# An adaLN block with a long convolution and a spatial gating MLP on one core: where the operand sets of the spatial product are built, stored and loaded

## The chip, the cores and the metric

The kernel runs on one core of a Trainium2 chip. The metric is the device time of one execution in microseconds; lower is better. Engines are named as in the profile: PE is TensorE's matmuls and PEld its weight loads, DVE is VectorE, ACT is ScalarE, POOL is GpSimd, SP is SyncE. SP, ACT and POOL also issue DMAs, each in its own queue, in order.

## The reference, cut to what matters

```python
x = A_u                                             # [1, 2048, 576], f32
sa, ca, ga, sb, cb, gb = (silu(c) @ w_mod), six rows of 576
h = layernorm(x) * (1 + ca) + sa
x = x + ga * ssm_convolution(h)                     # 128 states a channel, by FFT in the reference
h = layernorm(x) * (1 + cb) + sb
z = gelu(h @ w_in)                                  # w_in 576 x 4608
z1, z2 = z[:, :2304], layernorm(z[:, 2304:])
g = w_sp @ z2 + b_sp[:, None]                       # w_sp 2048 x 2048, the spatial product
x = x + gb * ((z1 * g) @ w_out)                     # w_out 2304 x 576
```

The change lies in the second half, from the second layernorm on.

## The kernel before, in words

**Numbers.** Each f32 operand of the large matmuls is split into two fp16 parts, hi and lo, and three products of parts stand for one product. Large products are made by a Strassen-like scheme with seven products of half-sized blocks in place of eight. It needs seven combined operands on either side, sums and differences of four quarter blocks, each as hi and lo.

**First stage (`phase_a`).** All 2048 rows, in 16 tiles b of 128, go through the second layernorm, are transposed on TensorE (`turn`), and multiplied with the z2 half of w_in (`z2_mm`, five column parts h). ScalarE applies the gelu (`z2_gelu`), statistics follow, the normalised z2 is stored to `z2_d` in HBM. The transposed tile lies in PSUM (`pt`, two banks, one buffer). `turn_hi` (ACT) and `turn_lo` (DVE) make its fp16 parts. For b of 4 and more `turn_lo` also copies all of it in f32 with ScalarE to `nf` (a single buffer, shown as `wf` in the profile) and stores that with three POOL DMAs to `nm_d` and `nr_d`, for the later blocks. In this stage every instruction keeps its written order on its engine (`self.nc = self.tied`).

**Second stage (`phase_b`).** Four blocks q of 512 output rows each. A block has nine units f of 256 columns of z. A unit makes z1 (`z1_unit` in block 0, `z1_pair` in blocks 1 to 3) and then the spatial product (`g_unit`, `g_products`) over four operand sets n = 4f to 4f+3 of z2, each multiplied with two of the eight tiles of w_sp of the block. A set has 14 fp16 tiles, 896 KB, in a ring of three buffers (`zset`). It takes 42 matmuls: for each of two w_sp tiles seven products of three parts, one part on each of lines L1586, L1587 and L1588. After the nine units DVE scales and adds the bias (`gt`), multiplies with z1, and `out_block` multiplies with w_out (L1638 to L1641).

**Operand sets.** `set_unit` either builds a set from z2 (`z2_build`: a load of 512 KB from `z2_d` on SP into `raw`, three sums on DVE, then hi on ACT, L1136, and lo on DVE, L1137, twice each) or loads it ready from `set_d` with a POOL DMA (L1563). `kept_in(n)` is 1 for every third set and 0 else. A set with 0 is built in block 0, stored to `set_d` by an ACT DMA (L1580) and loaded in blocks 1 to 3. A set with 1 is built in block 0 and again in block 1, stored in block 1, and loaded in blocks 2 and 3. `ready(q, n + 2)` asks for a set when set n starts.

**w_in's combined operands.** Blocks 1 to 3 need the z1 half of w_in as seven combined operands for each f (`wc`, `wcr`, one buffer each). `w_load(f)` reads w_in on SP into two `raw` buffers; `w_build(f)` makes them (eight sums and three lo parts on DVE, three hi parts on ACT) and stores them with two POOL DMAs (L1523, L1524) to `wc_d` and `wr_d`. In block 1 `w_build(f + 1)` follows `z1_pair(1, f)`; blocks 2 and 3 load them (`w_parts`). `w_load(0)` stands at the end of unit 7 of block 0, `w_build(0)` and `w_load(1)` in its unit 8, after `n_build` (which makes the combined operands of the transposed rows) and ahead of `g_unit(0, 8)`.

**w_sp of the next block.** `wsp_read` loads eight tiles of 512 KB on SP into `raw` (four buffers, shared by z2, w_in, w_sp, w_out, the transposed rows and x), `wsp_build` combines them, between the last unit and `out_block`.

**Order.** The kernel's framework schedules instructions on each engine itself, except where the helper `Mixed` or `tied` keeps the written order: SP always, DVE and ACT in unit 8 of blocks 0 to 2 and from the fourth `wsp_build` on. Lines of such instructions show as L133. POOL is never tied in this stage.

Of the kernel before, what the change touches and what calls it, by code (L numbers as in the profile page):

```python
# [800 lines left out]
class Mlp:  # L801
# [409 lines left out]
        A.activation(nt[:, 8], pm[:, 1, :128], AF.Copy)  # L1211

    def turn_lo(self, b):
        V, pm, nt = self.nc.vector, self.tps.pop(b), self.nts[b]
        V.tensor_tensor(nt[:, 4:8], pm[:, 0].rearrange("p (k c) -> p k c", k=4), nt[:, 0:4], op=ALU.subtract)
        V.tensor_tensor(nt[64:, 8], pm[64:, 1, :128], nt[64:, 8], op=ALU.subtract)
        if b < 4:
            self.nc.gpsimd.dma_start(self.n2_d[:, b], nt)
            return
        q, t, c = b // 4 - 1, b % 4 // 2, slice(128 * (b % 2), 128 * (b % 2) + 128)  # L1220
        nf = self.nf
        self.nc.scalar.activation(nf, pm.rearrange("p k n -> p (k n)")[:, :640], AF.Copy)
        self.nc.gpsimd.dma_start(self.nm_d[q, t, :, :, c], nf[:, :512].rearrange("p (k c) -> p k c", k=4))
        for h in range(2):
            self.nc.gpsimd.dma_start(self.nr_d[q, :, 2 * t + h, c], nf[32 * h:32 * h + 32, 512:])
# [39 lines left out]
    def phase_a(self):  # L1265
# [21 lines left out]
        def do(b, k):  # L1287
            for fn, a in sides[b][k]:
                fn(*a)
# [65 lines left out]
        for b in range(1, 16):  # L1355
            do(b, LD)
            self.z2_mm(b, 0)
            do(b, A0)
            self.z2_gelu(b, 0)
            self.z2_stats(b - 1, 5)  # L1360
            if b in (1, 2):
                do(b, PE)
                self.z2_mm(b, 1)
                self.turn(b + 1)
                self.z2_gelu(b, 1)
                self.turn_hi(b + 1)
                self.turn_lo(b + 1)
            self.roots(b - 1, b + 2 if b + 2 < 16 else None)
            if b % 2:
                self.z2_diff(b - 1)  # L1370
            self.z2_norm(b - 1)
            if b + 2 < 16:
                self.ln2_rows(b + 2)
            if b + 4 < 16:
                self.x1_load(b + 4)
            if b > 2:
                if b > 3:
                    do(b, PE)
                self.z2_mm(b, 1)
                if b + 1 < 16:  # L1380
                    self.turn(b + 1)
                self.z2_gelu(b, 1)
            self.z2_store(b - 1)
            do(b, V0)
            self.z2_stats(b, 0, 1)
            if 3 < b + 1 < 16:
                self.turn_hi(b + 1)
                self.turn_lo(b + 1)
            self.z2_mm(b, 2)
            if b == 3:  # L1390
                do(b, PE)
            self.z2_gelu(b, 2)
            do(b, A1)
            self.z2_mm(b, 3)
            self.z2_stats(b, 2, 3)
            self.z2_gelu(b, 3)
            if b + 3 < 16:
                self.ln2_stats(b + 3)
            do(b, V1)
            self.z2_stats(b, 4)  # L1400
            self.z2_mm(b, 4)
            self.z2_gelu(b, 4)
# [154 lines left out]

    def set_unit(self, n, q):

        if q <= self.kept_in(n):  # L1560
            return self.z2_build(n)
        o = self.bp.tile([128, 7, 2, 256], F16, name="zset", bufs=3)
        self.nc.gpsimd.dma_start(o, self.set_d[n // 4, n % 4])  # L1563
        return o

    def kept_in(self, n):
        return 1 if n % 3 == 2 else 0

    def g_products(self, q, f):

        T = self.nc.tensor
        p6, p32, p17, p54 = pg = [self.bank().rearrange("p (k n) -> p k n", k=2) for _ in range(4)]

        todo = [(5, 4, p6, 0), (6, 1, p32, 0), (3, 2, p32, 1), (1, 0, p17, 0), (0, 5, p17, 1), (4, 3, p54, 0), (2, 6, p54, 1)]
        for i in range(8):
            if i % 2 == 0:
                n = 4 * f + i // 2
                z = self.zset.pop((q, n))
                if q == self.kept_in(n):
                    self.nc.scalar.dma_start(self.set_d[f, i // 2], z)  # L1580
                self.ahead(q, n)
            w = self.wsp[q, i]
            c = slice(128 * (i % 2), 128 * (i % 2) + 128)
            for a, b, bank, half in todo:
                pm = bank[:, half]
                T.matmul(pm, z[:, a, 0, c], w[:, b, 0], start=i + half == 0, stop=False, skip_group_check=True)  # L1586
                T.matmul(pm, z[:, a, 0, c], w[:, b, 1], start=False, stop=False, skip_group_check=True)  # L1587
                T.matmul(pm, z[:, a, 1, c], w[:, b, 0], start=False, stop=i == 7, skip_group_check=True)  # L1588
        return pg
# [94 lines left out]
    def phase_b(self):  # L1684
# [2 lines left out]
        self.pb = self.pool(self.ctx, "pb", 8, space=PSUM)  # L1687
        self.bank = lambda: self.pb.tile([128, 512], F32, name="ps")
        self.zset = {}
        made = [n for n in range(36)], [n for n in range(36) if self.kept_in(n)], [], []  # L1690
        loaded = [0] * 4
        AHEAD = 3

        def more(q, n):

            while loaded[q] < min(n, len(made[q])):
                self.z2_load(made[q][loaded[q]])
                loaded[q] += 1

        def ready(q, n):  # L1700
            if n < 36:
                if n in made[q]:
                    more(q, made[q].index(n) + (AHEAD if q == 0 else 1))
                self.zset[q, n] = self.set_unit(n, q)

        blocks = [0] * 4
# [31 lines left out]
        bp.tile([128, 7, 2, 256], F16, name="zset", bufs=3)  # L1738
        bp.tile([128, D], F32, name="gbs")
        bp.tile([128, 288], F32, name="ot", bufs=2)  # L1740
        more(0, AHEAD)
        self.wsp_read(self.raw(("b", 7)), 0, 7)
        ready(0, 0)
        for i in range(2, 6):
# [4 lines left out]
        for q in range(4):  # L1749
            done = 0  # L1750

            def z1(n):
                nonlocal done
                while done < min(n, 18):
                    self.z1_unit(q, order[done])
                    done += 1

            for f in range(9):
                if f == 8 and q < 3:
                    self.scales_sp(q + 1, self.bank())  # L1760
                    self.scales_gate(q + 1)
                if q == 0:
                    if f == 5:
                        self.scales_in(self.bank())
                    z1(units(q, f))
                else:
                    self.z1_pair(q, f)
                    if q == 1 and f < 8:
                        self.w_build(f + 1)
                        if f < 7:  # L1770
                            self.w_load(f + 2)
                    elif q > 1 and f < 8:
                        self.w_parts(f + 1)
                if f == 8 and q < 3:
                    if q == 0:
                        self.cfp.close()
                        self.parts_open()
                    self.nc, plain = Mixed(self.tc, self.tied, self.tied), self.nc
                    self.n_build()
                    if q == 0:  # L1780
                        self.w_build(0)
                        self.w_load(1)
                    else:
                        self.w_parts(0)
                    self.nc = plain
                self.g_unit(q, f)
                if q == 0:
                    if f == 5:
                        for i in (6, 7):
                            self.wsp_load(1, i, None)  # L1790
                            self.norm_sp(1, i)
                elif q < 3 and f < 6:
                    for i in ((0, 1), (2, 3), (4,), (5,), (6,), (7,))[f]:
                        self.wsp_load(q + 1, i, None)
                        self.norm_sp(q + 1, i)
                if f == 6 and q < 3:
                    self.sums_sp(q + 1)
                if f == 6:
                    self.load_gate(q)
                if q == 0 and f == 3:  # L1800
                    self.sums_in()
                if f == 7 and q < 3:
                    self.n_load(q + 1)
                    if q == 0:
                        self.w_load(0)
            self.scale_gate(q)
            if q < 3:
                for i in range(8):
                    if i == 3:
                        self.nc, plain = Mixed(self.tc, self.tied, self.tied), self.nc  # L1810
                    self.wsp_build(q + 1, i)
                    block(q + 1, i + 5)
                self.nc = plain
                self.bias_load(q + 1)
                ready(q + 1, 0)
                ready(q + 1, 1)
            self.out_block(q)
# [85 lines left out]
```

## Time and profile before

| | us |
|---|---|
| median of 3 runs | 1806.05 |
| lowest and highest | 1804.48, 1806.15 |
| profiled execution | 1803.76 |
| its span | 1801.9 |

| engine | busy in the span |
|---|---|
| PE | 1690.0 us, 94% |
| PEld | 1255.6 us, 70% |
| DVE | 1253.0 us, 70% |
| ACT | 848.0 us, 47% |
| POOL | 246.8 us, 14% |

Within the span, the first stage of the MLP ends near 690 us. The spatial products of the four blocks start at 694.76, 971.74, 1270.22 and 1536.76 us. An x and a number behind a busy time is the count of instructions. "Idle before" is how long an engine stood still just ahead of an instruction, and the arrow names what ended that. The granted clock is TensorE's, 1.00 being full speed.

### The profile page before, as it was taken

Reading aid. Unit: us, or ns where it says so; the run is one execution under the profiler, and the core shown is the slowest. Engines: PE = TensorE matmul, PEld = TensorE weight load, DVE = VectorE, ACT = ScalarE, POOL = GpSimd, SP = SyncE. Lnnn points to the kernel's source line nnn. Section 1 sums busy time; section 2 is a strip of 40 time slices with the busy share of each in tenths; the row PEclk is TensorE's granted clock in tenths of the full one; section 3 lists DMA queues with packets and bytes.
Section 4 is the critical chain, followed back from the end, with each engine's and each line's share of the span. In section 5 each row is a group of like instructions: output and inputs, shape, how many; then the busy total and the mean of one; then the engine's idle time right before and its main releaser. Section 6 shows DMA issues by size and latency. Waiting matters only on the chain. (4 is left out here: it accounts for less than half of the span.)

```text
span 1801.9 us, 35541 instructions
## 1 busy us (share of the span) xinstructions
PE 1690.0 (94%) x14771; PEld 1255.6 (70%) x14771; DVE 1253.0 (70%) x2365; ACT 848.0 (47%) x1084; POOL 246.8 (14%) x392
## 2 busy tenths in 40 slices
PE   5687999997999999999989889899999999999999
PEld 1344555564545547777767778787888887888887
DVE  6997999866888888996976658687344467344432
ACT  4778999944577675554532434343122133111110
POOL 2221222332133220000000001000000000000000
PEclk9898999997999999999999999999999999999999
DMA  8457455799598788876545567673666682555620
GB/s 274 141 201 250 133 140 167 196 252 284 177 301 272 243 238 270 296 278 225 191 168 202 211 261 255 253 269 122 214 227 225 216 285 76 181 210 195 234 91 27
DMA packets 148368, 380.67 MB, mean 211 GB/s; under 512 B 24160, under 2 KB 61984, under 8 KB 146672
## 3 DMA queue, kind: packets, MB, share of 16 engines
q1 hardware_dynamic: 103104, 176.49, 31.4%
q0 software_dynamic: 35616, 163.76, 26.9%
q10 hardware_dynamic: 9488, 38.16, 5.2%
q8 instruction: 116, 1.90, 0.4%
q14 instruction: 44, 0.36, 0.1%
HBM read 266.05 MB, written 102.86 MB: 205 GB/s over the span
## 5 line engine op out<-in xcount | busy, mean ns | idle before, releaser
L1586 PE MATMUL ps<-wsp,zset 128*128 128x256 f16 x2016 | 553.5, 275 | 22.4 <-ACT zset L1136 13.9
L1588 PE MATMUL ps<-wsp,zset 128*128 128x256 f16 x2016 | 552.1, 274 | 3.2 <-DVE zset L1137 3.2
L1587 PE MATMUL ps<-wsp,zset 128*128 128x256 f16 x2016 | 553.1, 274 | 0.0
L1586 PEld LDWEIGHTS <-zset 128*128 128x128 f16 x2016 | 198.7, 99 | 50.4 <-ACT zset L1136 16.2
L133 PE MATMUL pz<-wz,nt 128*128 128x512 f16 (+1 forms) x1120 | 224.0, 360 | 2.3 <-ACT nt L133 1.9
L1588 PEld LDWEIGHTS <-zset 128*128 128x128 f16 x2016 | 198.4, 98 | 29.2 <-DVE zset L1137 5.1
L1587 PEld LDWEIGHTS <-zset 128*128 128x128 f16 x2016 | 198.7, 99 | 25.0
L1601 DVE SCALAR_TENSOR_TENSOR gt<-ps,sc,bsp 128x512 f32<-128x512 f32 x33 | 24.8, 750 | 251.9 <-PE ps L1588 251.9
L133 PEld LDWEIGHTS <-nt 128*128 128x128 f16 x1120 | 109.6, 99 | 108.4 <-ACT nt L133 3.5
L1563 POOL DMA_DIRECT2D zset<-set_d x96 | 50.8, 529 | 835.3 <-PE ps L1588 580.3
L1638 PE MATMUL ps<-wout,z 128*128 128x288 f16 x448 | 125.4, 289 | 6.7 <-DVE gt L133 4.7
L1640 PE MATMUL ps<-wout,z 128*128 128x288 f16 x448 | 128.3, 289 | 1.4 <-DVE gt L133 1.4
L1641 PE MATMUL ps<-wout,z 128*128 128x288 f16 x448 | 128.3, 289 | 0.0
L1550 ACT ACTIVATE z<-ps 128x512 f32<-128x512 f32 x21 | 12.5, 597 | 229.6 <-PE ps L1543 229.6
L1601 DVE SCALAR_TENSOR_TENSOR gt<-ps,sc,gt 128x512 f32<-128x512 f32 (+1 forms) x165 | 112.0, 696 | 5.2 <-DVE gt L1601 0.5
L1540 PE MATMUL ps<-nq,wc 128*128 128x256 f16 x378 | 103.1, 273 | 0.0
L1542 PE MATMUL ps<-nq,wc 128*128 128x256 f16 x378 | 103.1, 273 | 0.0
L1541 PE MATMUL ps<-nq,wc 128*128 128x256 f16 x378 | 102.9, 272 | 0.0
L1136 ACT ACTIVATE zset<-raw 128x1024 f16<-128x1024 f32 x48 | 50.3, 1050 | 98.1 <-DMA raw<-z_d 33.7
L1137 DVE TENSOR_TENSOR zset<-raw,zset 128x1024 f16<-128x1024 f32 x48 | 58.7, 1223 | 29.5 <-ACT zset L1136 29.5
L133 DVE BATCH_NORM_STATS2 bsz<-z 128x6 f32<-128x384 f32 x96 | 48.5, 547 | 17.3 <-ACT z L133 17.3
L1640 PEld LDWEIGHTS <-z 128*128 128x128 f16 x448 | 44.2, 99 | 18.0 <-DVE gt L133 6.6
(410 smaller groups left out, 3374.6 us busy)
## 6 DMA issues: line engine op xcount, KB each, us to landing
zset<-set_d POOLq DMA_DIRECT2D x96, 896.0 KB, 4.9
set_d<-zset ACTq DMA_DIRECT2D x36, 896.0 KB, 6.2
raw<-z_d SPq DMA_DIRECT2D x48, 512.0 KB, 5.0
raw<-in_w_spT SPq DMA_DIRECT2D x43, 512.0 KB, 5.8
z_d<-z POOLq DMA_DIRECT2D x32, 576.0 KB, 7.8
wc<-wc_d SPq DMA_DIRECT2D x18, 896.0 KB, 4.8
u_d<-st1o POOLq DMA_DIRECT2D x16, 576.0 KB, 4.8
u<-u_d SPq DMA_DIRECT2D x36, 256.0 KB, 4.8
```

Source lines behind the costliest of these rows:

```text
L133: return self.tc.keep_in_program_order(f(*a, **k))
L1137: nc.vector.tensor_tensor(o[:, k, 1], t, o[:, k, 0], op=ALU.subtract)
L1540: T.matmul(pm, w[0], n[0], start=c + half == 0, stop=False, skip_group_check=True)
L1541: T.matmul(pm, w[0], n[1], start=False, stop=False, skip_group_check=True)
L1542: T.matmul(pm, w[1], n[0], start=False, stop=False, skip_group_check=True)
L1586: T.matmul(pm, z[:, a, 0, c], w[:, b, 0], start=i + half == 0, stop=False, skip_group_check=True)
L1587: T.matmul(pm, z[:, a, 0, c], w[:, b, 1], start=False, stop=False, skip_group_check=True)
L1588: T.matmul(pm, z[:, a, 1, c], w[:, b, 0], start=False, stop=i == 7, skip_group_check=True)
L1601: V.scalar_tensor_tensor(dst, pm, inv, to, op0=ALU.mult, op1=ALU.add)
L1638: T.matmul(pl, p[:, 1, ts], w[:, 0, hs], start=st, stop=sp)
L1640: T.matmul(pa, p[:, 0, ts], w[:, 0, hs], start=st, stop=False)
L1641: T.matmul(pa, p[:, 0, ts], w[:, 1, hs], start=False, stop=sp)
```

## The change

`set_unit` builds sets in block 0 only, all 36 are stored there by ACT DMAs, and blocks 1 to 3 load all of theirs with POOL DMAs; `kept_in` goes. `w_load(0)`, `w_build(0)` and `w_load(1)` move from units 7 and 8 of block 0 into and behind the loop of `wsp_build` for block 1, that is, behind all eight loads of w_sp on SP and behind the seventh `wsp_build`. The f32 copy of the transposed tile and its three stores leave `turn_lo` for a function `turn_out`, which is called after the fourth gelu of the tile before.

```diff
@@ turn_lo
-        V, pm, nt = self.nc.vector, self.tps.pop(b), self.nts[b]
+        V, pm, nt = self.nc.vector, self.tps[b], self.nts[b]
...
         if b < 4:
             self.nc.gpsimd.dma_start(self.n2_d[:, b], nt)
+
+    def turn_out(self, b):
+        if b < 4 or b > 15:
             return
+        pm = self.tps.pop(b)
         q, t, c = b // 4 - 1, b % 4 // 2, slice(128 * (b % 2), 128 * (b % 2) + 128)
         nf = self.nf
         self.nc.scalar.activation(nf, pm.rearrange("p k n -> p (k n)")[:, :640], AF.Copy)
@@ phase_a
             self.z2_stats(b, 2, 3)
             self.z2_gelu(b, 3)
+            self.turn_out(b + 1)
             if b + 3 < 16:
                 self.ln2_stats(b + 3)
@@ set_unit
-        if q <= self.kept_in(n):
+        if q == 0:
             return self.z2_build(n)
         o = self.bp.tile([128, 7, 2, 256], F16, name="zset", bufs=3)
         self.nc.gpsimd.dma_start(o, self.set_d[n // 4, n % 4])
         return o
-
-    def kept_in(self, n):
-        return 1 if n % 3 == 2 else 0
@@ g_products
-                if q == self.kept_in(n):
+                if q == 0:
                     self.nc.scalar.dma_start(self.set_d[f, i // 2], z)
@@ phase_b
-        made = [n for n in range(36)], [n for n in range(36) if self.kept_in(n)], [], []
-        loaded = [0] * 4
+        loaded = 0
         AHEAD = 3
-        def more(q, n):
-
-            while loaded[q] < min(n, len(made[q])):
-                self.z2_load(made[q][loaded[q]])
-                loaded[q] += 1
+        def more(n):
+            nonlocal loaded
+            while loaded < min(n, 36):
+                self.z2_load(loaded)
+                loaded += 1
         def ready(q, n):
             if n < 36:
-                if n in made[q]:
-                    more(q, made[q].index(n) + (AHEAD if q == 0 else 1))
+                if q == 0:
+                    more(n + AHEAD)
                 self.zset[q, n] = self.set_unit(n, q)
...
                     self.n_build()
-                    if q == 0:
-                        self.w_build(0)
-                        self.w_load(1)
-                    else:
+                    if q > 0:
                         self.w_parts(0)
...
                 if f == 7 and q < 3:
                     self.n_load(q + 1)
-                    if q == 0:
-                        self.w_load(0)
...
                     self.wsp_build(q + 1, i)
                     block(q + 1, i + 5)
+                    if q == 0 and i == 3:
+                        self.w_load(0)
+                    if q == 0 and i == 6:
+                        self.w_build(0)
+                if q == 0:
+                    self.w_load(1)
```

More of the change, by code (lines that the diff above doesn't have):

```diff
@@ L1740, in phase_b @@
         bp.tile([128, 288], F32, name="ot", bufs=2)
-        more(0, AHEAD)
+        more(AHEAD)
         self.wsp_read(self.raw(("b", 7)), 0, 7)
```

## The prediction

> **What bounds the kernel now.** I read the page first, then the stages in windows, then the same point in three blocks, then TensorE's waits in the second one. In the window rows the columns are: stretch, its length, busy time of PE, PEld, DVE, ACT and POOL, granted clock, DMA share, GB/s.
>
> ```profile
> span 1801.9 us, 35541 instructions
> 460.00:690.00 230.00, 224.65 (x1182) 116.22 (x1182) 193.99 (x540) 159.60 (x234) 65.47 (x88) 1.00 0.79 244
> 690.00:883.00 193.00, 188.91 (x1543) 150.50 (x1542) 169.01 (x270) 98.83 (x120) 0.00 (x0) 1.00 0.76 265
> 883.00:972.00 89.00, 80.07 (x651) 64.18 (x649) 71.50 (x132) 36.28 (x45) 2.20 (x4) 0.96 0.44 149
> 972.00:1215.00 243.00, 222.22 (x1931) 191.83 (x1929) 171.12 (x286) 93.86 (x108) 21.23 (x40) 0.96 0.70 252
> 1262.00:1485.00 223.00, 223.00 (x2034) 198.50 (x2032) 101.48 (x160) 50.72 (x63) 19.01 (x36) 1.00 0.68 234
> ```
>
> The rows are the stage that makes z2, the first block's body, its end, the second block and the third. TensorE bounds all of them: in the third block it never rests, in the others little. So the most that a change off TensorE can bring is TensorE's idle time and its lost clock, and these lie in the second block and ahead of it. How much the second block has too much is told by the distance between the first spatial product of blocks two, three and four:
>
> ```profile
> 971.74 0.27 PE L1586 MATMUL ps<-wsp,zset 128*128 128x256 f16 x1
> 1270.22 0.27 PE L1586 MATMUL ps<-wsp,zset 128*128 128x256 f16 x1
> 1536.76 0.27 PE L1586 MATMUL ps<-wsp,zset 128*128 128x256 f16 x1
> ```
>
> Second to third 298.5 us, third to fourth 266.5, with the same matmuls in both: 31.9 us too much. What TensorE and the builders waited for between 972 and 1215 (busy, mean ns, idle before, and what ended it):
>
> ```profile
> L1586 PE MATMUL ps<-wsp,zset 128*128 128x256 f16 x503 | 141.2, 281 | 19.1 <-ACT zset L1136 13.1 <-DMA zset<-set_d 5.1 <-DVE gt L1601 0.8
> L1588 PE MATMUL ps<-wsp,zset 128*128 128x256 f16 x502 | 139.7, 280 | 1.7 <-DVE zset L1137 1.7
> L1137 DVE TENSOR_TENSOR zset<-raw,zset 128x1024 f16<-128x1024 f32 x12 | 14.7, 1223 | 18.3 <-ACT zset L1136 18.3
> L1136 ACT ACTIVATE zset<-raw 128x1024 f16<-128x1024 f32 x12 | 12.7, 1057 | 68.9 <-DMA raw<-z_d 33.7 <-DMA set_d<-zset 27.8 <-PE ps L1588 7.3
> ```
>
> Waits sum to 20.8 us; the clock row of 0.96 over 243 us is 9.7 us more. Together 30.5 of the 31.9. Of the waits 14.8 are for rebuilt sets, whose ScalarE half itself stood 33.7 us for the z2 load and 27.8 for a store that still held a buffer; 5.1 is one wait for a loaded set. A short gap also costs clock: here the gap, then the stretch behind it.
>
> ```profile
> 980.80:983.50 2.70, 0.66 (x5) 0.11 (x2) 2.67 (x4) 1.53 (x2) 0.55 (x1) 1.00 1.04 434
> 983.50:986.90 3.40, 3.23 (x16) 2.30 (x17) 2.00 (x7) 0.00 (x0) 0.00 (x0) 0.51 1.03 388
> ```
>
> Two microseconds of gap, then 3.4 us at half clock, 1.7 us lost.
>
> **The second block without builds.** Twelve builds go, with their z2 loads, vector and scalar work, and twelve stores; twelve set loads on the GpSimd queue come instead. Nothing is left that TensorE could wait for but loaded sets. In the third block 36 of them cost nothing; in the second the landings are slower:
>
> ```profile
> L1563 POOL DMA_DIRECT2D zset<-set_d x22: 527/528/549, 976.9 to 1185.7; - x22
> DMA to landing us min/median/max: 4.8/8.1/11.1
> L1563 POOL DMA_DIRECT2D zset<-set_d x36: 527/527/537, 1275.3 to 1478.9; - x36
> DMA to landing us min/median/max: 4.5/4.9/7.8
> ```
>
> First pair second block, second pair third. What differs is the traffic and, in the GpSimd queue, two stores of w_in's operands per unit of four sets:
>
> ```profile
> 1008.28 0.53 POOL L1524 DMA_DIRECT2D wr_d<-wcr  x1 [1.00 <-DVE wcr L1522]
> 1008.80 0.53 POOL L1563 DMA_DIRECT2D zset<-set_d  x1
> 1031.45 0.27 PE L1586 MATMUL ps<-wsp,zset 128*128 128x256 f16 x1
> 1037.10 0.54 POOL L1523 DMA_DIRECT2D wc_d<-wc  x1 [10.04 <-DVE wc L839]
> 1038.62 0.53 POOL L1524 DMA_DIRECT2D wr_d<-wcr  x1 [0.98 <-DVE wcr L1522]
> ```
>
> The load at 1008.80 has no idle time before it: it was queued behind the stores, which wait for VectorE, and it is the one that TensorE waited 5.1 us for. It is the last set of its unit (its buffer comes free after the unit's first set); in this kernel a third of these sets were built, now all are loaded. A set's 42 matmuls take 4.6 us (223 us over 2034 matmuls, times 42), so it is due 13.8 us after its unit starts. The unit at 1031.45 shows when the queue is free: 1038.62 + 0.53, 7.7 us in. That leaves 6.1 us for a landing. The bounds: the third block's median, 4.9, stalls nothing; the second's maximum, 11.1, stalls 5.0 us and half a clock stretch, 6.7 us in each of units 1 to 7, 47 us. I take the value nearest by place, the second block's median with its bytes scaled:
>
> ```profile
> DMA packets 12756, 56.99 MB, mean 250 GB/s; under 512 B 1436, under 2 KB 1532, under 8 KB 12737
> set_d<-zset ACTq DMA_DIRECT2D x11, 896.0 KB, 8.1
> raw<-z_d SPq DMA_DIRECT2D x11, 512.0 KB, 7.1
> ```
>
> Out go 11 stores and 11 z2 loads (15.9 MB), in come 11 set loads (10.1 MB): 51.2 of 57.0 MB, so 7.3 us and a stall of 1.2 in units 1 to 5, which also read w_sp for the next block; 0.3 each in units 6 and 7, which don't; one half-clock stretch for all, 1.7. Sum 8.3: the second block gains 31.9 - 8.3 = 23.6.
>
> By the Trainium skill (TensorE: Matmul & The Clock Gate, What's actually happening) the clock falls after an idle window of some 3.4 us; stalls of 1.2 us would then cost no clock and the sum would be 1.7 us lower. The trace's half stretch behind a shorter gap speaks for leaving the 1.7 in.
>
> **The end of the first block.** Here w_in's first operands are built ahead of the last unit's sums, and their loads stand ahead of the next block's w_sp.
>
> ```profile
> 890.23 0.36 SPq L133 DMA_DIRECT2D raw<-in_w  x1
> 903.36 1.05 SPq L133 DMA_DIRECT2D raw<-in_w_spT  x1
> 912.32 0.42 DVE L1081 TENSOR_TENSOR sum<-raw 128x256 f32<-128x256 f32 x1 [4.66 <-DMA raw<-in_w_spT]
> PE ps L1638 <- DVE gt L133: 4.7, 1, 4.7
> PE ps L1640 <- DVE gt L133: 1.4, 1, 1.4
> PE ps L1638 <- ACT ot L1648: 2.0, 1, 2.0
> 918.70:925.50 6.80, 5.42 (x23) 3.30 (x23) 5.08 (x9) 1.98 (x2) 0.00 (x0) 0.50 0.63 245
> 896.60:902.90 6.30, 6.30 (x54) 5.02 (x53) 6.22 (x14) 2.18 (x2) 0.54 (x1) 1.00 0.31 107
> ```
>
> SyncE's four w_in loads stand between 890.23 and 903.36; moved behind the w_sp loads they let the first w_sp block go 13 us sooner. VectorE's 4.66 us wait at 912.32, with the gate sums (gt) queued behind it, then has its data, and the sums also come sooner by w_build(0), about 5.5 us of VectorE time (last row, less two small operations of a set build). So the gt waits, 6.1, and half of 6.8 us at half clock, 3.4, go: 9.5. Moved, the 5.5 us stand ahead of the output sums, which free the banks that cost the 2.0; VectorE's lost wait pays for most of it, and I leave 0.5 for the rest: 9.0 gained. Bounds: all three waits and the clock, 11.5, and nothing, if VectorE's work only changes order. Its two GpSimd stores move with it, past the first set loads of the second block, which have tens of microseconds; w_in's second pair is loaded after the loop, ahead of the row loads on SyncE, and is used only when the second block starts. These I cost at nothing.
>
> **The first block's body.** Twelve more stores of 896 KB on ScalarE's queue. Each set's buffer is built again three sets later, so the store must land within that time.
>
> ```profile
> L1580 ACTq DMA_DIRECT2D set_d<-zset x23: 326/327/359, 689.7 to 877.0; - x23
> DMA to landing us min/median/max: 4.1/5.7/9.1
> ```
>
> Landing 9.1 at worst against 13.8 or more, and issue 12 x 0.33 = 4 us on a ScalarE with half its time free. But 11 MB join a stage at 265 GB/s. Bounds: nothing, and 41 us if every byte added time. The 23 stores now there live beside 4.1 us of TensorE idle in all; half of that for twelve more would be 2, and I take 1.
>
> **The copy behind the fourth gelu.** ScalarE loses its wait for VectorE there:
>
> ```profile
> ACT wf L133 <- DVE nt L133: 19.4, 12, 2.8
> 590.51 1.04 ACT L133 ACTIVATE z<-pz,sc 128x512 f32<-128x512 f32 x2
> 594.97 0.27 PE L133 MATMUL pt<-ident,n 128*128 128x128 f32 x1
> ```
>
> ScalarE isn't the bound; TensorE's idle time in this stage is 5.4 us, the upper bound of the gain, and I take 2. The moved copy (0.7 us) holds the transpose's banks longer: after the fourth gelu, the first of the pair at 590.51, it ends near 592, and the next transpose is at 594.97. A loss starts beyond those 3 us; lower bound 0 to -1. Its three GpSimd stores pass no other GpSimd instruction.
>
> **Sum:** -23.6 - 9.0 + 1 - 2 = -33.6, say -33. The profiled execution took 1803.8 us (span and 1.9 around it), which gives 1771. The runs' median is 2.3 higher, so **1773**.
>
> **Rivals.**
> 1. The sets land in time: the queue takes the load ahead of the stores, or landings come near the third block's 4.9. The 8.3 goes: 1764.
> 2. Landings stay at the second block's 8.1: 2.0 and 1.7 in seven units, 26 instead of 8.3: about 1790. For it: stores of w_in and w_sp loads stay. Against it: a tenth of the bytes goes.
> 3. The other side: the GpSimd queue becomes the bound. If each of seven last sets waits like the one behind the stores (5.1) plus a half-clock stretch of 6.8 us, 8.5 in all, that is 59 against 31.9 removed: +27 - 10 = about 1823; at 6.7 each 1811. It turns slower than before from 42 / 7 = 6 us per unit. One load in this trace did that; others of its place did not stop TensorE.
> 4. The first block pays for the stores: a third of the 41 us, 14 instead of 1: 1786. Against: TensorE is 98% busy there.
> 5. GpSimd's descriptors are held up by VectorE: every set load waits for two VectorE operations ahead of it (1223 ns each in the row of the set builds), 2.4 us in seven tight units, 17 more: 1790. Against: the issues last 527 to 549 ns in the busy block and 527 to 537 in the calm one, so no trace of it. The Trainium skill (SBUF — State Buffer, SBUF: two separate sides) warns of this: a DMA issued from GpSimd can wait while a VectorE operation holds the port they share, 620 ns becoming 3100.
>
> **How the numbers follow.** Forecast 0.55 (its own range 1766 to 1782), rival 1 0.18, rival 2 0.13, rival 3 0.04, rival 4 0.08, rival 5 0.02. 1760 to 1790 holds the first two, most of rival 4 and half of rivals 2 and 5: over 0.8. A measurement of this kernel tells 0.2% (3.6 us) from nothing. Only rival 3 ends slower: 0.04; 0.01 for no change, 0.95 faster.
>
> **What would show it.** From first product to first product the second block takes about 275 us, not 298; no TensorE wait for ACT or DVE zset in it; waits for set_d of about a microsecond, at the last set of a unit, each behind a wr_d store. At the first block's end no 4.7 us gt wait and no half clock near 920. ScalarE's copy waits for nothing. Wrong it would be by long set_d waits, over 5 us of TensorE idle time in the first block's body, or a later bank wait for the output sums.

## The result, and the profile after

The changed kernel takes 1798.8 us (median of 11 runs, 1788.8 to 1804.9) against 1808.9 before (11 runs on the same chip): a ratio of 0.994, 95% interval 0.992 to 0.996. That is 10 us faster where 33 were forecast. The profiled execution is the fastest of the eleven, 1788.8 us.

The window rows of the changed kernel, for the first block's body, its end, the second block and the third (columns as in the prediction; units are counted from 0):

```profile
span 1787.0 us, 35474 instructions
...
690.00:883.00 193.00, 190.33 (x1578) 153.81 (x1577) 166.46 (x266) 101.30 (x121) 0.00 (x0) 1.00 0.84 303
883.00:972.00 89.00, 82.63 (x683) 67.41 (x682) 71.27 (x133) 32.58 (x39) 4.90 (x9) 0.96 0.57 197
972.00:1215.00 243.00, 220.55 (x1950) 191.89 (x1949) 143.56 (x236) 75.51 (x87) 25.54 (x48) 0.98 0.61 226
1262.00:1485.00 223.00, 223.00 (x2022) 197.45 (x2021) 111.12 (x172) 56.68 (x68) 18.56 (x35) 1.00 0.67 233
```

VectorE and ScalarE lost the work that was to go in the second block (171 to 144 and 94 to 76 us), and the moved bytes fell from 252 to 226 GB/s. TensorE is no busier there than before. The first spatial products of blocks two, three and four stand at:

```profile
960.80 0.27 PE L1588 MATMUL ps<-wsp,zset 128*128 128x256 f16 x1
...
1255.60 0.27 PE L1588 MATMUL ps<-wsp,zset 128*128 128x256 f16 x1
...
1522.14 0.27 PE L1588 MATMUL ps<-wsp,zset 128*128 128x256 f16 x1
```

Second to third 294.8 us, third to fourth 266.5 as before: 28.3 us too much are left of 31.9. TensorE's waits in the second block and in the first (total, times, longest):

```profile
PE ps L1588 <- DMA zset<-set_d: 22.4, 8, 4.4
...
PE ps L1640 <- ACT ot L1650: 6.2, 1, 6.2
PE ps L1590 <- DVE zset L1137: 2.7, 3, 1.6
```

The waits for rebuilt sets are gone, and so are those for the gate sums. In their places stand eight waits for loaded sets, one in each of the first eight units, and a single long one for the output sums. GpSimd's queue in unit 2, whose first product is at 1014.41:

```profile
1020.06 0.54 POOL L1528 DMA_DIRECT2D wc_d<-wc  x1 [10.04 <-DVE wc L839]
1021.58 0.53 POOL L1529 DMA_DIRECT2D wr_d<-wcr  x1 [0.98 <-DVE wcr L1527]
1022.11 0.53 POOL L1568 DMA_DIRECT2D zset<-set_d  x1
1024.04 0.53 POOL L1568 DMA_DIRECT2D zset<-set_d  x1 [1.39 <-PE ps L1590]
```

The place is exactly the one that the prediction named: the unit's last set is queued behind the `wr_d` store and leaves 7.7 us into the unit. What differs is the landing of this load (transfers issued at 1022.11: size, us to landing):

```profile
zset<-set_d POOLq DMA_DIRECT2D x1, 896.0 KB, 10.6
```

Over the units 1 to 6 it is 9.7, 10.6, 8.4, 9.3, 9.6 and 9.6 us, with 6.1 us at hand. Three of the eight waits cost clock too; one of them, and the stretch behind it:

```profile
1000.00:1002.50 2.50, 0.00 (x0) 0.00 (x0) 0.00 (x0) 0.00 (x0) 0.39 (x1) 1.00 1.02 419
1002.50:1005.90 3.40, 2.86 (x14) 2.05 (x15) 0.00 (x0) 0.00 (x0) 0.00 (x0) 0.50 1.01 412
```

Three stretches of 3.4 us at half clock are 5.1; with 22.4 of waits they make 27.5 of the 28.3.

At the first block's end, VectorE's order, then the sum that TensorE waits for:

```profile
928.41 0.42 DVE L133 TENSOR_TENSOR sum<-raw 128x256 f32<-128x256 f32 x1
...
933.04 1.14 DVE L133 SCALAR_TENSOR_TENSOR wcr<-raw,sc,wcr 32x896 f16<-32x896 f32 x1
...
937.20 1.28 DVE L133 SCALAR_TENSOR_TENSOR wsp<-sum,sc,wsp 128x1024 f16<-128x1024 f32 x1
939.01 0.83 DVE L1660 TENSOR_TENSOR raw<-ot,raw 128x288 f32<-128x288 f32 x2 [0.53 <-DMA raw<-x_d]
...
939.56 0.41 ACT L1650 ACTIVATE ot<-ps 128x288 f32<-128x288 f32 x1 [2.40 <-DVE raw L1660]
```

`w_build(0)` runs from 928.41 to 934.2, the last `wsp_build` to 938.5, and only then come the output sums that free TensorE's banks.

### The profile page after: what moved, and what is told of

The parts are those of the page before. It is cut to its first block, busy times and chain, and to the rows that moved or that the text cites. A ratio compares the mean times of both kernels' runs of the same rounds, so it can differ in the third digit from the quotient of the medians.

```text
span 1787.0 us, 35474 instructions
## 1 busy us (share of the span) xinstructions
PE 1675.8 (94%) x14771; PEld 1251.7 (70%) x14771; DVE 1220.0 (68%) x2305; ACT 827.8 (46%) x1060; POOL 257.6 (14%) x404
## 4 chain that ended last, share of the span: by engine, by line
PE 52%; DVE 12%; DMA 8%; issue 8%; ACT 2%; POOL 1%; SPq 0%; ACTq 0%; POOLq 0%; DVEq 0%
PE pz L133 9%; PE ps L1588 8%; PE ps L1589 8%; PE ps L1590 8%; DMA zset<-set_d 4%; PE ps L1643 3%; PE ps L1640 3%; PE ps L1642 3%; DVE zset L1137 2%; DVE gt L1603 2%; PE ps L1545 2%; PE ps L1547 2%; PE ps L1546 2%; DMA raw<-z_d 1%; PE ps L1548 1%
## 5 line engine op out<-in xcount | busy, mean ns | idle before, releaser
L1588 PE MATMUL ps<-wsp,zset 128*128 128x256 f16 x2016 | 551.5, 274 | 22.6 <-DMA zset<-set_d 22.4
L1568 POOL DMA_DIRECT2D zset<-set_d x108 | 57.4, 531 | 837.2 <-PE ps L1590 581.5
L371 PE MATMUL ps<-ln_x,r1t 128*128 128x288 f32 x128 | 42.0, 484 | 22.8 <-ACT kab L439 9.9
L133 ACT ACTIVATE z<-pz,sc 128x512 f32<-128x512 f32 (+1 forms) x80 | 50.7, 640 | 23.5 <-PE pz L133 19.9
L1650 ACT ACTIVATE ot<-ps 128x288 f32<-128x288 f32 x32 | 12.9, 409 | 95.8 <-PE ps L1640 76.4
```

The source lines that it names most:

```text
L133: return self.tc.keep_in_program_order(f(*a, **k))
```

## The experiments

The names of the theories in the expectations: Q says that the place behind w_in's stores in GpSimd's queue makes the loads late, T that the block's traffic does, O that the output sums wait for `w_build(0)`. The two mends are: w_in's stores of block two out of the way of the set load, and `w_build(0)` late.

All kernels were timed beside the kernel before (its medians in those groups are 1809.8 to 1810.6). "To block one" is the time of the first spatial product, "block one" and "block two" the distances from it to that of the next block, all from one profiled execution. The third block took 266.5 to 267.9 in every kernel.

| kernel | to block one | block one | block two | median us | ratio to before (95%) |
|---|---|---|---|---|---|
| before | 694.8 | 277.0 | 298.5 | 1808.9 | 1 |
| the change | 688.8 | 272.0 | 294.8 | 1798.8 | 0.994 (0.992 to 0.996) |
| sets alone | 694.9 | 284.6 | 303.0 | 1813.5 | 1.001 (0.998 to 1.003) |
| w_in alone | 695.9 | 271.5 | 300.8 | 1803.7 | 0.997 (0.995 to 0.998) |
| copy alone | 690.8 | 272.3 | 310.5 | 1800.0 | 0.994 (0.992 to 0.996) |
| sets and copy | 691.6 | 278.9 | 304.3 | 1804.7 | 0.998 (0.996 to 1.000) |
| w_in and copy | 689.8 | 270.0 | 310.3 | 1800.1 | 0.993 (0.991 to 0.995) |
| change, stores on SyncE | 698.8 | 282.3 | 269.3 | 1778.7 | 0.981 (0.978 to 0.983) |
| change, stores cut | 687.9 | 273.8 | 266.5 | 1763.5 | 0.973 (0.971 to 0.975) |
| change, w_build(0) late | 687.4 | 267.2 | 306.9 | 1797.1 | 0.993 (0.990 to 0.995) |
| change, small store ahead (1) | 688.7 | 275.9 | 275.7 | 1775.7 | 0.982 (0.980 to 0.985) |
| change, small store ahead (2) | 691.8 | 278.3 | 282.2 | 1784.1 | 0.985 (0.984 to 0.987) |
| change, stores behind the set | 687.7 | 278.2 | 272.4 | 1771.0 | 0.979 (0.976 to 0.982) |
| both mends, SyncE | 689.4 | 267.9 | 270.0 | 1761.2 | 0.973 (0.970 to 0.976) |
| both mends, behind the set | 689.7 | 266.7 | 278.8 | 1769.7 | 0.979 (0.976 to 0.981) |
| both mends, sets rebuilt | 689.5 | 267.5 | 325.8 | 1810.5 | 1.000 (0.999 to 1.002) |

A block's time in one profile is that of one execution, and those of one kernel differ (the change took 1788.8 to 1804.9): block two is 294.8 in the change and 303.0 with the sets alone, with the same work in that block and the same waits for sets (22.4 and 22.6). With rebuilt sets it is 298.5 and 300.8 without the moved copy and 310.5 and 310.3 with it; whether the copy has a part in this is not shown. Verdicts below on a few us rest on the ratios, not on one profile.

**The parts.** Each part put into the kernel before by itself, and two pairs.

```diff
 sets alone     if q <= self.kept_in(n):  ->  if q == 0:      (z2_load, g_products alike)
 w_in alone     w_load(0), w_build(0), w_load(1) moved among the wsp_builds, as in the change
 copy alone     turn_out(b + 1) called behind z2_gelu(b, 3)
```

> Only the first part: all 36 sets stored by the first block and loaded by the second; w_in's operands and the copy of tile rows stay as before. Theory Q (the last set of a unit is issued behind w_in's two stores and lands in 9.3 to 10.6 us instead of the predicted 7.3): the second block, first product to first product, shrinks from 298.5 to about 295, 20 to 24 us of idle time for set_d stay in it, and the whole is 3 to 5 us faster than before. The prediction's term for this part, 23.6 less 1, would make it 22 us faster; that falls if it gains under 10.

> Only the second part: w_in's first operands made after the w_sp loads. The two traces at hand give about 5 us for this part (from first product of block one to that of block two, 277.0 before and 272.0 after, part of which may belong to the sets). Theory O (the waits for gate sums go, and a wait for the output sums of about 6 us with a half-clock stretch takes their place): 3 to 6 us faster, waits for gt under 1 us, the wait for ot about 6 us. The prediction's term: 9.0 us faster, with the wait for ot at about 2.5. The second block, with its rebuilt sets, unchanged at 298 within 2.

> Only the third part: the copy of tile rows behind the fourth gelu. Predicted 2 us; the changed kernel's trace shows TensorE's gaps between 440 and 700 us at 2.5 instead of 5.8 us, so 3.4. Expected 2 to 4 us faster, all of it ahead of the first spatial product (before: 694.8). The rival, a delayed transpose, would show as a wait of TensorE for the pt banks and no gain.

> The change without its second part (w_in's operands as before). If the parts add: the sum of the gains of the two alone, 5 to 9 us faster than before by theory Q, 25 by the prediction's terms. Set beside the full change (10 us faster by the medians) it also gives the second part's worth on top of the other two: theory O expects 3 to 6 us, the prediction's term 9.

The sets alone bring nothing: 1.001, where 0.988 was forecast for this part. Their profile has the same eight waits as the full change:

```profile
PE ps L1583 <- DMA zset<-set_d: 22.6, 8, 4.6
```

w_in alone brings 0.35% (6 us), the upper end of theory O's 3 to 6; no wait for gate sums is left at the block's end (2.8 us lie at 857, where the kernel before has them too), and the output sums wait 5.2 us, as it said. The copy alone brings 0.6%, 7 to 15 us, above the 2 to 4 expected. ScalarE's wait for VectorE ahead of the copy falls from 19.4 to 0.2 us, as forecast. In the profiles only 4.0 us of the gain lie ahead of block one and 4.7 more in block one; the pair without and with the copy beside the sets shows much the same (3.3 and 5.7), the pair beside w_in 6.1 and 1.5. A reason for the gain in block one may be seen in how long the set builders' ScalarE half waits for TensorE in the 120 us around block one's start, first of the kernel before, then with the copy moved, then with sets and copy:

```profile
ACT zset L1136 <- PE ps L1588: 1.4, 1, 1.4
```

```profile
ACT zset L1136 <- PE ps L1593: 12.7, 6, 2.8
```

```profile
ACT zset L1136 <- PE ps L1590: 22.0, 12, 2.8
```

A builder that waits for TensorE is ahead of it (the buffer that it wants is still being multiplied). With the old copy the builders enter block one late and TensorE runs into them; with the moved one they enter ahead. In seven profiles (before, the change, the parts and the pairs) the wait is 1.4 to 3.2 us in the three without the moved copy and 12.7 to 22.0 in the four with it. That the head start causes the gain in block one is likely but not shown by itself.

**Queue or traffic.** Two edits of `w_build`'s stores.

```diff
 stores on SyncE
-        nc.gpsimd.dma_start(self.wc_d[f], o)
-        nc.gpsimd.dma_start(self.wr_d[f], p)
+        nc.sync.dma_start(self.wc_d[f], o)
+        nc.sync.dma_start(self.wr_d[f], p)
 stores cut, for f > 0
+            nc.gpsimd.dma_start(self.wc_d[0, :, 6:, 1], o[:, 6:, 1])
+            nc.gpsimd.dma_start(self.wr_d[0, :, 6], p[:, 6])
```

> The changed kernel with w_in's two stores per unit issued by SyncE instead of GpSimd; same bytes, and the last set of a unit no longer queued behind them: it is issued about 3 us earlier, when its buffer comes free, 9.2 us ahead of its use. Theory Q (the queue is the cause, and the crowding behind it makes the slow landings): landings fall to about 5, waits for set_d in the second block from 22.4 to under 5 us, half-clock stretches there go, the second block takes 267 to 272 us and the whole is 20 to 30 us faster than the changed kernel. Theory T (the traffic of the block is the cause): landings stay at 9.3 to 10.6, so 0.1 to 1.4 us per unit are left, about 5 to 8 us of waits, and the whole is 12 to 18 us faster than the changed kernel.

> The changed kernel with seven of eight pairs of w_in's stores cut to a fourteenth and a seventh of their bytes (the later blocks read the first pair instead, so the output is not the reference's); number of issues, their waits for VectorE and the queue order stay. The last set of a unit is still issued 7.7 us into it, 6.1 ahead of its use. Theory T: with 7 MB less written, landings of these loads fall to 5 to 6 us, and the waits for set_d go from 22.4 to under 4 us; 20 us or more faster than the changed kernel. Theory Q: three set loads still leave within 6 us of one another, landings stay above 8 us, and 2 to 4 us per unit (15 us or more in all) stay; under 8 us faster.

On SyncE the waits for sets fall from 22.4 to 0.4 us, block two takes 269.3 with no half-clock stretch, and the last sets of units 2 to 8 land in 4.9 to 6.1 us (unit 1's in 9.2, issued in time): theory Q's numbers. Its waits, in the second block, then at the end of the first:

```profile
PE ps L1588 <- DVE gt L1603: 1.6, 2, 0.8
PE ps L1588 <- DMA zset<-set_d: 0.4, 1, 0.4
...
PE ps L1640 <- ACT ot L1650: 10.1, 1, 10.1
```

The last row is a cost of this version: the first pair's stores now stand on SyncE ahead of the x tiles that the output sums need. The kernel with cut stores leaves out nearly all of seven pairs of operands, and the later blocks read the first pair in their place, so its output is another. It does not tell the theories apart. With smaller stores the framework put the set load between them:

```profile
987.55 0.55 POOL L1532 DMA_DIRECT2D wc_d<-wc  x1 [6.52 <-DVE wc L839]
990.46 0.53 POOL L1572 DMA_DIRECT2D zset<-set_d  x1 [2.37 <-PE ps L1594]
992.58 0.53 POOL L1533 DMA_DIRECT2D wr_d<-wcr  x1 [1.59 <-DVE wcr L1527]
```

So queue order and bytes changed together, and the 35 us gained over the change are worth no more than a bound on the two.

**Late, or behind the stores' data.** Stores on SyncE, and in their place on GpSimd a store of 8 KB ahead of the unit's last set, which keeps that load late but not behind 1.06 MB. `tied` keeps the written order.

```diff
+            if q == 1 and n % 4 == 1 and n < 32:
+                self.tied.gpsimd.dma_start(self.hold_d[f], self.wcr[:32, 6])      # (1)
+                self.tied.gpsimd.dma_start(self.hold_d[f], self.wcr[32:64, 6])    # (2)
             ready(q, n + 2)
```

> The changed kernel with w_in's stores of the second block issued by SyncE (the first pair stays on GpSimd), and a small store of 8 KB of the same operand put on GpSimd's queue in their place, ahead of the last set of each unit: the bytes and the late issue (7.7 us into the unit, 6.1 ahead of use) stay, but that load no longer stands behind 1.06 MB of stores in its own queue. Theory Q1 (the load is slow because its data follow the stores' data in the same queue): it lands in 5 to 6 us, waits for set_d in the second block under 3 us, block two 267 to 270 us. Theory Q2 (late issue crowds three set loads and the block's other traffic): landings of 8 to 10 us stay and so do 2 to 4 us of wait per unit, block two 285 or more.

> As the kernel with the small store held in GpSimd's queue, but the small store now reads rows 32 to 64 of the operand, which VectorE writes last; there it held the set load back in three units only. Now every last set is issued 7 us or more into its unit, 6.1 to 6.8 ahead of use, behind 8 KB instead of 1.06 MB. Theory Q1 (data behind the stores' data in the same queue): landings 5 to 6.5 us, waits for set_d under 4 us, block two 267 to 275 us, within 6 us of the kernel with the earlier small store. Theory Q2 (lateness and crowding): landings 8 us or more, 2 to 4 us of wait in each of units 1 to 7, block two 285 or more.

In (1) the rows read were ready early and the load was late (7.4 us into the unit) in three units only; it landed there in 5.9, 5.0 and 6.0 us. No wait for sets is left in (1); its block two has 6.2 us of waits for gate sums. In (2) the load is late in every unit from 1 to 7. Its queue in one unit, the landing of that load, and TensorE's waits in the block:

```profile
1030.58 0.52 POOL L133 DMA_DIRECT2D hold_d<-wcr  x1 [11.55 <-DVE wcr L1528]
1031.10 0.56 POOL L133 DMA_DIRECT2D zset<-set_d  x1
```

```profile
zset<-set_d POOLq DMA_DIRECT2D x1, 896.0 KB, 7.8
```

```profile
PE ps L1590 <- DMA zset<-set_d: 12.8, 7, 4.0
```

Units 2 to 7 land in 7.1 to 8.1 us, unit 1 in 10.2. This is between the theories: Q1 said under 6.5 and under 4 us of waits, Q2 said above 8 and block two at 285 or more; it is 282.2. So both have a part. Medians over units 1 to 7: issued late and behind the stores in one queue, 9.6 us (the change); late, behind 8 KB, 7.8; in time, with the stores on SyncE, 5.1.

The packets of GpSimd's queue show the two parts. They carry no names, but counted off in order, 128 of 7168 bytes for each transfer of 896 KB, they come out even in the three runs compared here. In the change, from 1015 to 1026.8, this queue (packets, MB, share) moved the 896 KB of `wc_d` and nothing else, though the load was issued at 1022.11:

```profile
q0 software_dynamic: 143, 0.92, 20.3%
```

The packets of `wr_d` start between 1026.89 and 1028.57, the load's first one at 1027.30. Over units 1 to 6 the load's first packet starts 4.5 to 5.6 us after the issue in the change, 1.9 to 2.3 in (2), and 1.2 with the stores on SyncE (2.7 in unit 1). From there to the landing it takes 3.8 to 5.4 us in the change and 5.1 to 7.9 in (2). So the load's data do stand behind the stores' data in the queue, some 3 us. A late load that need not wait for them starts sooner but moves more slowly. That fits the crowding of theory Q2: in (2) the next set load is issued 1.9 to 2.6 us behind it, but 3.4 to 5.2 us behind it in the three late units of (1), where the landings were shorter. The crowding was not varied by itself.

By the Trainium skill (DMA: Bandwidth & Descriptors, Queues, rings and completion order) each DMA engine serves the queue rows in turn, a packet at a time, and takes the descriptors of one row in ring order, which that section states of SyncE's and ScalarE's rows. By that, if GpSimd's row is served alike, a load behind 1.06 MB in its own row waits for them, and one on another row shares. The first packets, 4.5 to 5.6 us and 1.9 to 2.3 us after the issue, agree.

**Order alone.** The stores stay on GpSimd, issued behind the unit's last set load.

```diff
             ready(q, n + 2)
+            if q == 1 and n % 4 == 1 and n < 32:
+                self.w_store()
```

> The changed kernel with w_in's two stores per unit still on GpSimd's queue, but issued behind the last set load of the unit instead of ahead of it. Bytes and queue the same, order alone changed. Theory Q: the last set is issued 5 us into its unit and lands in time, waits for set_d under 4 us, block two 267 to 272 us, 20 to 30 us faster than the changed kernel. If the traffic of the stores is the cause whatever their order: loads of the next unit, behind the stores, land late instead, 10 us of waits or more stay, 10 us faster at most.

Block two takes 272.4 and no TensorE wait for a loaded set is left; 28 us faster than the change by the medians, as theory Q said. The slow landing has not gone, it has moved: the next load behind the stores, the following unit's first set, now takes 7.6 to 11.0 us, but it is issued 13 to 17 us ahead of its use.

**The first block's end.** `w_build(0)` and `w_load(1)` after the fourth output sum.

```diff
                     A.dma_start(self.out[b], xts[tt])
+            if q == 0 and n == 3:
+                self.w_build(0)
+                self.w_load(1)
```

> The changed kernel with w_in's first operands made after the fourth of the eight output sums instead of ahead of all of them (and its second pair loaded there). Theory O (the 6.2 us wait for the output sums at the end of the first block, with its 6.8 us at half clock, is w_build's VectorE time ahead of them): the wait falls to under 1.5 us, the half-clock stretch goes, first product to first product of block one 264 instead of 272, and the whole 5 to 9 us faster than the changed kernel. Rival: VectorE is as late from the w_sp builds alone: wait stays at 4 or more, under 3 us gained; or the operands come late for the second block's first pair, a wait for wc, and nothing is gained.

The wait for the output sums goes (rows of block one, then of block two):

```profile
PE ps L1590 <- DVE zset L1137: 3.6, 3, 1.6
PE ps L1588 <- ACT zset L1136: 1.5, 2, 1.2
PE ps L1588 <- ACT z1b L1441: 0.7, 1, 0.7
PE ps L1642 <- DVE ot L1658: 0.3, 1, 0.3
...
PE ps L1588 <- DMA zset<-set_d: 29.9, 8, 5.7
```

Block one falls from 272.0 to 267.2, with no half-clock stretch at its end, and is as short (266.7 to 267.9, none at the end) in each of the three later kernels with this edit. So theory O holds, but the whole can't be told from the change (0.993 and 0.994): the waits for sets rose to 29.9. Most of the 7.5 us more are in unit 0: the stores of unit 1's operands now leave 9.5 and 10.7 us into it, still ahead of its last set, which TensorE waits 5.7 us for (1.0 in the change).

**The change without its sets, and the two mends together.**

> The change without its first part: sets as before (twelve rebuilt in the second block), w_in's operands later, copy moved. The parts alone measured 6.8 (w_in) and 10.5 (copy) faster, the sets 3 slower to 1.5 faster in what they add. If the parts add: 15 to 17 us faster than before, 4 to 7 faster than the full change. The prediction's terms say the opposite: 22 us slower than the full change.

> Two mends together: w_in's stores of the second block on SyncE, and the first operands made after the fourth output sum (their stores on GpSimd). If both mechanisms hold, block one takes 264 to 268 us and block two 267 to 271, and the whole is 1758 to 1768 us, 30 to 40 faster than the changed kernel. Rival: the late operands delay the second block's first pair and the wait moves there: block two 275 or more.

> The same two mends, with the stores on GpSimd behind the unit's last set load instead of on SyncE. The same time as with SyncE, within 4 us, if only the order in GpSimd's queue matters; slower by 10 or more if a queue shared with the stores is a cost of its own.

> The best version so far (w_in's stores of the second block on SyncE, first operands after the fourth output sum, copy moved), but with the sets as before the change: twelve rebuilt in the second block, 24 loaded. If the stored sets are what the mended queue pays for: the rebuilt sets still wait for z2 loads and buffers, block two 285 to 300 us, the whole 15 to 30 us slower than the best version. If the queue alone was the cause of all of block two's excess: block two 270 to 278 and the whole within 6 us of the best version.

w_in and copy without the sets: 0.993, not told from the full change; 13 us faster, with an interval of 8 to 17, so whether the parts add up to the 15 to 17 us expected stays open. With and without the stored sets the ratio is 1.001 and 1 (alone), 0.998 and 0.994 (beside the copy), 0.994 and 0.993 (beside both): as the change has them they gain nothing, and may cost up to 7 us. The two mends with the stores on SyncE (the first pair on GpSimd) are the best version, 1761.2 us (1756.9 to 1763.5): 49 us faster than before and 38 faster than the change, within what was expected. Its waits, in block two and ahead of it:

```profile
PE ps L1589 <- DVE gt L1604: 2.3, 2, 1.5
PE ps L1589 <- DMA zset<-set_d: 0.4, 1, 0.4
...
PE ps L1591 <- DVE zset L1137: 0.6, 1, 0.6
PE ps L1643 <- DVE ot L1659: 0.3, 1, 0.3
```

With the stores behind the set instead it is 8.5 us slower, not within 4: hardly a wait for sets (0.6), but 5.2 us for gate sums, 2.2 for an output sum and a half-clock stretch of 6.8 us, so this order has a cost of its own that I have not traced further. With the sets rebuilt, all the gain is gone (1.000; 49 us slower than the best version, where 15 to 30 were expected):

```profile
PE ps L1592 <- ACT zset L1136: 43.3, 8, 10.1
...
ACT zset L1136 <- DMA raw<-z_d: 43.4, 5, 13.1
```

The rebuilt sets wait for their z2 loads, which are on SyncE, and there the moved stores now stand among them; so this run shows that the best version needs the stored sets, but not what the rebuilt ones would do with the stores elsewhere.

## Why the prediction was wrong, point by point

**The second block: 23.6 forecast, 3.7 seen.** Mechanism, place, issue time (7.7 us) and due time (13.8) were right, and the term that failed is the landing: "the second block's median with its bytes scaled ... 7.3". As a median that was right (7.4 over the block's loads). But the load that TensorE waits for is not a median load: it stands directly behind the stores, and landed in 9.6. The trace of before had the row, four times: loads issued within 0.6 us behind a `wr_d` store. Two of them:

```profile
zset<-set_d POOLq DMA_DIRECT2D x1, 896.0 KB, 9.8
...
zset<-set_d POOLq DMA_DIRECT2D x1, 896.0 KB, 9.4
```

The other two took 9.5 and 9.1. Three of the four did not stop TensorE, and the prediction counted that against rival 3. But they were in time only because TensorE had waited 2.2, 3.3 and 3.8 us for a rebuilt set just before: the loads of units 0, 3 and 6 landed at 986.4, 1076.8 and 1153.6, while 13.8 us into the unit are 985.5, 1073.8 and 1150.3. The waits that the change removes had hidden the ones that it keeps. With 9.45 the step gives 3.35 us of stall in seven units, 23.5, near the 22.4 of the profile. The median is pulled down by loads such as the unit's third set, which leave late in the unit before (4.7 to 5.4 us in the profile after). What decided between 8.3 and 28.3 us was thus two microseconds in one number, taken eight times, and the clock that followed.

**Half clock.** One stretch of 1.7 us was taken for the block, three came, 5.1. They are not fixed by the length of the stall: of the six waits of 2.8 to 4.4 us three cost a stretch and three did not. The clock records tell them apart. All stretches start on a grid of 3.41 us (in the profile of before the one at 983.5 and the one at 1017.7 are ten steps apart), and what counts is TensorE's idle time within one step. In all sixteen profiles, between the first products of blocks one and four, each of the 72 beginnings of half clock follows a step with 1.94 us or more of idle time (by the matmuls' ends in the profile, which are modelled), and only three other full-clock steps have that much (1.97 to 2.00). The 2.8 us wait in unit 3 had 2.26 us in one step and cost a stretch; the 3.5 us in unit 5 fell as 1.66 and 1.83 into two steps and cost none (step, length, PE busy first; the clock is the last but two):

```profile
1057.13:1060.54 3.41, 1.15 (x11) 0.78 (x8) 1.52 (x4) 0.00 (x0) 0.53 (x1) 1.00 1.02 425
1060.54:1063.95 3.41, 2.84 (x14) 2.05 (x15) 0.00 (x0) 0.00 (x0) 0.00 (x0) 0.50 1.00 420
...
1111.74:1115.15 3.41, 1.75 (x17) 1.31 (x14) 1.22 (x4) 0.00 (x0) 0.53 (x1) 1.00 1.05 426
1115.15:1118.57 3.42, 1.59 (x15) 1.44 (x16) 0.30 (x1) 0.00 (x0) 0.00 (x0) 1.00 1.00 421
```

So the forecast's stalls of 1.2 us would have cost no clock, and stalls of 3.5 us cost none or some by where they fall. Three other kernels whose block two has the same stores ahead of the same loads lost 11.9 us of clock there (`w_build(0)` late), 13.7 (sets and copy) and 15.4 (sets alone). The profiled execution of the change, the fastest of eleven, was lucky with its 5.1; that this is what separates it from the median is likely but not shown.

By the Trainium skill (TensorE: Matmul & The Clock Gate, What's actually happening) the window is 3413 ns and free-running. The grid agrees. By the same section of the Trainium skill the clock falls after an idle window of that length; the steps above differ, about 2.0 us of idle time within one were enough.

**The end of the first block: 9.0 forecast.** That the gate sums stop waiting was right. The wrong term is the 0.5 for `w_build(0)`'s 5.5 us ahead of the output sums: they wait 6.2 us and a 6.8 us stretch at half clock returns, 3.4 more. VectorE pauses there for no more than 0.5 us at a time, so what is put ahead of the output sums delays them; with `w_build(0)` behind the fourth of them the wait is 0.3. The part is worth 6 us by itself.

**The copy: 2 forecast, about 10 seen by itself.** Its direct part (4 us ahead of block one) was near. Missed was a gain in block one, most likely because builders who enter it ahead stay ahead.

**The stores: 1 forecast.** The body of block one shows 2.7 us of waits, so they are no 14 (rival 4). Four pairs of profiles with and without them differ by 0 to 8 us in block one, where five kernels with the same block one as the change spread by 6; this stays open.

**The rivals.** Rival 2's 26 us came nearest to the 28.3, for a reason half right: its 8.1 is a median too, with 2.0 of stall where 3.5 were seen (mean of units 1 to 6), and a half-clock stretch in all seven units where three had one. Rival 3, on the other side, names the same wait at 8.5 us a unit; it was 3.5 (28.3 / 8, clock included). Rival 5 is not needed: with the same VectorE work beside them, loads issued in time and with no store in their queue landed in 5 us. The profiled execution, 1788.8, lies inside the range and the median, ten us above it, does not; the forecast of 1771 for an execution like the profiled one missed both, because a median stood where the landing in that very place was needed.

## What to carry to other kernels

When one transfer decides a stage, take its landing from the transfers in the same place of the same queue, not from the stage's median. That such a transfer stopped nothing before the change proves little if another wait, which the change removes, stood in front of it. A load with little time to spare should not share a queue with stores that wait for an engine; the same bytes one queue over, or behind it in order, were worth 20 to 28 us here. And where an engine is full, work moved on it is only moved: ask what stands behind it in the new place.

## What the runs showed of the hardware

A load of 896 KB landed in 5.1 us when issued in time with no stores in its queue, in 7.8 when late, and behind 1.06 MB of stores in its own queue in 9.6 (medians of seven units; the ranges are 4.9 to 9.2, 7.1 to 10.2 and 6.7 to 10.6). Behind the stores its first packet started 4.5 to 5.6 us after the issue, else 1.2 to 2.7 (units 1 to 6). While three set loads were in flight together the DMA engines moved 412 to 419 GB/s in 2.5 to 3.4 us stretches, with the block's mean at 226, so the mean did not show how crowded the moments were that counted.

And the clock fell to half when TensorE had stood idle for about 2.0 us (1.94 to 2.00 is the edge) within one step of a fixed grid of 3.41 us. So a stall of 2.8 us cost a stretch and one of 3.5 us, split by the grid, cost none in the same block of one execution.
